# Column sums of w_out: 32 products with ones on TensorE, or 31 additions on VectorE and one product

## The chip, the cores and the metric

One core of a Trainium2 chip. The time is the device time of one execution in microseconds (us). Three runs of the kernel before gave 987.38 us as their median (986.65 to 991.73).

## The reference

Attention over 8 batches of 576 tokens with 8 heads of width 64 gives `x` with 4608 rows of 512. A feed-forward part follows, and the change lies in it:

```python
h = x @ w_in                        # 512 -> 2048
r = np.maximum(h, 0.0)
g = s * (r * r) + b                 # s and b are single numbers
return (g @ w_out).astype(np.float32)   # 2048 -> 512
```

Since `b` is one number, `g @ w_out` is `s * ((r*r) @ w_out)` plus a row of 512 that is the same for every token: `b` times the column sums of `w_out`. The kernel computes this row once, as the tile `bias`.

## The kernel before

`w_in` and `w_out` arrive as 64-bit floats. `split_w(p)` loads the part of them that belongs to f pair `p` (256 of the 2048 hidden columns, `p` = 0 to 7) and turns every number into a high and a low part: `wi[p]` and `wo[p]`. The tile `wo[p]` is 128 partitions by 2 (high, low) by 2 by 512, so it holds four pieces of 128x512. The tokens are tiled in 18 blocks `t` of 256, and each has a high and a low part `xh`, `xl`.

A step `(t, p)` has two halves. `gemm1(t, p)` does 24 products of 256 columns into the PSUM tile `ph` (lines 544 to 546). Then ScalarE does relu, square and a rounded copy `gh` (lines 554 to 556), and VectorE subtracts to get the rest `gl` (line 557). `gemm2(t, p)` does 12 products of 512 columns into two banks `po` (line 582 and 583 use `gh`, line 584 uses `gl`). It comes two steps later in the program, three from `t` = 3 on. In steps 14 to 23 every `ph` lies in bank 4, so the next `gemm1` can begin only when `gl` of the step in front has been read out of `ph`.

The steps run in the order of the list `order`: first `p` = 0 to 6 for `t` = 0 and 1 (steps 0 to 13), then `p` = 0 to 6 for `t` = 2 (steps 14 to 20), then `p` = 7 for the three (steps 21 to 23), then `t` = 3 to 17. The splits of the weights stand at the steps in `CONVERT_AT`, the last one (`p` = 7) at step 11. The attention of later batches is a generator that is advanced by `advance` between the steps. Its head pairs of batches 0 to 2 (`first_unit`) use `sa`, `sl`, `tp`, `tr`, `up` and `ol` products on TensorE, `L382` to `L400` and `L423` on VectorE and `L403` copies on ScalarE; `L271` waits for the load of `tqk`. From batch 3 on `local_unit` loads `lqk` and multiplies on GpSimd (line 455). A scheduler then places all instructions on the engines' queues, and each queue is worked off in that order.

`column_sums` is called ahead of `gemm2(0, 7)`: 32 products of a tile of ones with the pieces of all eight `wo[p]`, added up in bank 5 (`cs`, line 563), so that each of the 128 rows of `cs` holds the column sums. Line 565 multiplies by `b`. The outputs of a block `t` are `s * po + bias` (line 594; line 589 for the last block).

Of the kernel before, what the change touches and what calls it, by code (L numbers as in the profile page):

```python
# [10 lines left out]
F32 = mybir.dt.float32  # L11
F32R = mybir.dt.float32r
# [3 lines left out]
ALU = mybir.AluOpType  # L16
AX = mybir.AxisListType

P = 128
# [18 lines left out]
NFP = DFF // 256  # L38
# [14 lines left out]
HF = 7  # L53
# [8 lines left out]
def attention_ffn_kernel(ctx, tc, qk, vw_in, vr_in, vdm, qkn, vn, w_in, w_out, s_in, b_in, out):  # L62
    nc = tc.nc
    PS = bass.MemoryType.PSUM

    cst = ctx.enter_context(tc.tile_pool(name="cst", bufs=1))
# [4 lines left out]
    def bank(i, shape, name):  # L71
        return ps.tile(shape, F32, tag=f"k{i}", name=name)
# [90 lines left out]
    QV = NQ * 2 * GQ + P  # L163


    ones = cst.tile([P, P], F32R, name="ones")
    nc.gpsimd.memset(ones.bitcast(F32), 1.0)
    bias = cst.tile([P, DM], F32, name="bias")
    eps = cst.tile([P, 1], F32, name="eps")
    nc.gpsimd.memset(eps, 4e-9)  # L170
# [20 lines left out]
    wi, wo, wst = {}, {}, {}  # L191
# [4 lines left out]
    def load_w(p):  # L196

        parts = (("i", src_i[:, :, 512 * p : 512 * p + 512]), ("o", src_o[:, 2 * p : 2 * p + 2]))
        for op, src in parts:
            st = one.tile([P, 1024, 2], I32, tag=f"w{op}{STAGE[p]}", name="wst")  # L200
            nc.sync.dma_start(st.rearrange("p (k f) t -> p k (f t)", k=src.shape[1]), src)
            wst[(p, op)] = st
# [32 lines left out]
    def split_w(p):  # L235
        with tc.high_priority(offset=-BEHIND.get(p, 0)):
            split_parts(p)
# [279 lines left out]
    def split_x(t):  # L517
        tags = ("os", "xl2") if t == 2 else ("xh", "xl")
        pool = one if t == 2 else two
        xh = pool.tile([P, HP, TB], F32R, tag=tags[0], name="xh")  # L520
        xl = pool.tile([P, HP, TB], F32R, tag=tags[1], name="xl")
        t0 = t * TB
        while t0 < (t + 1) * TB:
            b = t0 // S
            while (b, HP - 1) not in complete:
                next(gen)
            n = min((t + 1) * TB, (b + 1) * S) - t0
            src = xt[b][:, :, t0 - b * S : t0 - b * S + n]
            dst = slice(t0 - t * TB, t0 - t * TB + n)
            nc.scalar.copy(xh[:, :, dst], src)  # L530
            nc.vector.tensor_tensor(
                xl[:, :, dst], src, xh[:, :, dst].bitcast(F32), ALU.subtract)
            t0 += n
        xs[t] = (xh, xl)
# [4 lines left out]
    def gemm1(t, p):  # L539
        xh, xl = xs[t]  # L540
        ph = bank(6 if t >= 3 and p % 2 else 7 if t == 1 and p < HF else 4, [P, 2, TB], "ph")
        for j, k in itertools.product(range(2), range(NK)):
            f = slice(P * j, P * j + P)
            nc.tensor.matmul(ph[:, j], wi[p][:, 0, k, f], xh[:, k], start=(k == 0), stop=False)  # L544
            nc.tensor.matmul(ph[:, j], wi[p][:, 0, k, f], xl[:, k], start=False, stop=False)  # L545
            nc.tensor.matmul(ph[:, j], wi[p][:, 1, k, f], xh[:, k], start=False, stop=(k == NK - 1))  # L546
        if t >= 3 and p % 3 == 2:
            both = one.tile([P, 2, 2, TB], F32R, tag="xl2", name="gb")
            gh, gl = both[:, 0], both[:, 1]
        else:  # L550
            gh = two.tile([P, 2, TB], F32R, tag="gh", name="gh")
            gl = two.tile([P, 2, TB], F32R, tag="gl", name="gl")
        with tc.high_priority():
            nc.scalar.activation(ph, ph, AF.Relu)  # L554
            nc.scalar.activation(ph, ph, AF.Square)  # L555
            nc.scalar.copy(gh, ph)  # L556
            nc.vector.tensor_tensor(gl, ph, gh.bitcast(F32), ALU.subtract)  # L557
        gt[(t, p)] = (gh, gl)

    def column_sums():  # L560
        cs = bank(5, [P, DM], "cs")
        for p, i in itertools.product(range(NFP), range(4)):
            nc.tensor.matmul(cs, ones, wo[p][:, i // 2, i % 2],
                             start=(p + i == 0), stop=(p == NFP - 1 and i == 3))
        nc.vector.tensor_scalar(bias, cs, sb_b, None, ALU.mult)

    def gemm2(t, p):
        if (t, p) == (0, NFP - 1):
            column_sums()
        gh, gl = gt.pop((t, p))  # L570
        if p == 0:
            ob = OB.get(t, OB[0])
            oacc[t] = [bank(i, [P, DM], "po") for i in ob]
        po = oacc[t]
        end = t == NB - 1 and p == NFP - 1
        os_ = one.tile([P, 2, DM], F32, tag="os", name="os") if p == NFP - 1 else None
        for m in range(2):
            ms = slice(P * m, P * m + P)
            for j in range(2):
                first = p == 0 and j == 0  # L580
                last = p == NFP - 1 and j == 1
                nc.tensor.matmul(po[m], gh[:, j, ms], wo[p][:, 0, j], start=first, stop=False)  # L582
                nc.tensor.matmul(po[m], gh[:, j, ms], wo[p][:, 1, j], start=False, stop=False)  # L583
                nc.tensor.matmul(po[m], gl[:, j, ms], wo[p][:, 0, j], start=False, stop=last)  # L584
            if end:
                r0 = TB * t + P * m
                for c in (0, DM // 2):
                    cs = slice(c, c + DM // 2)
                    nc.vector.scalar_tensor_tensor(
                        os_[:, m, cs], po[m][:, cs], sb_s, bias[:, cs], ALU.mult, ALU.add)  # L590
                    nc.sync.dma_start(out[r0 : r0 + P, cs], os_[:, m, cs])
        if p == NFP - 1 and not end:
            for m in range(2):
                nc.vector.scalar_tensor_tensor(
                    os_[:, m], po[m], sb_s, bias, ALU.mult, ALU.add)
            nc.sync.dma_start(
                out[TB * t : TB * t + TB, :].rearrange("(m p) c -> p m c", p=P), os_)
# [63 lines left out]
    def advance(st):  # L661
        nonlocal done
        while done < target(st):
            with tc.high_priority(offset=300 if done < NY[1] else 60 if done < NY[1] + NY[2] else 0):
                if next(gen, "end") == "end":
                    break
            done += 1
# [3 lines left out]
    at_step = {st: p + 1 for p, st in enumerate(CONVERT_AT)}  # L671
    for st, (t, p) in enumerate(order):
        gemm1(t, p)
        if st in at_step:
            split_w(at_step[st])
            if at_step[st] + 2 < len(STAGE):
                load_w(at_step[st] + 2)
        advance(st + 0.5)
        pend.append((t, p))
        if len(pend) > (2 if t < 3 else 3):  # L680
            gemm2(*pend.pop(0))
        advance(st + 1)
        if (t, p) in splits:
            split_x(splits[t, p])
# [64 lines left out]
```

## Time and profile before

| what | value |
|---|---|
| median of three runs | 987.38 us |
| profiled execution, its own time | 985.35 us |
| its span (first to last instruction) | 983.5 us |
| TensorE busy | 950.9 us (97%) |
| VectorE busy | 621.6 us (63%) |
| ScalarE busy | 478.0 us (49%) |
| GpSimd busy | 419.0 us (43%) |
| mean granted TensorE clock | 0.989 |

Times inside the execution are counted from the start of the span. PE is TensorE, DVE is VectorE, ACT is ScalarE, POOL is GpSimd and SP issues loads and stores. Matmuls overlap: the record of one is longer than the distance to the next one's start, so the cost of a row of products is read from the distance of the starts. A number in square brackets at the end of a row of the timeline is the idle time of the engine ahead of that row, with what ended it.

### The profile page before, as it was taken

The numbers are of one execution on the slowest core, as the hardware profiler recorded it, in microseconds if no ns is written. First come the engines' busy times: TensorE is split into PE (matmuls) and PEld (weight loads), VectorE is DVE, ScalarE is ACT, GpSimd is POOL, SyncE is SP. The second block draws the span as 40 slices with busy tenths as digits, with TensorE's granted clock in tenths as the row PEclk, the third lists the DMA queues.
The fourth block names the chain that finished last, engine by engine and source line by source line (L and its number), as shares of the span: only waits on it lengthen the run. The fifth ranks groups of instructions, "written<-read, shape, count | busy, mean of one in ns | idle before, by whom it ended". The sixth has DMA issues, their size and how long they took to land.

```text
span 983.5 us, 18562 instructions
## 1 busy us (share of the span) xinstructions
PE 950.9 (97%) x7346; PEld 850.8 (87%) x7346; DVE 621.6 (63%) x1144; ACT 478.0 (49%) x1141; POOL 419.0 (43%) x455
## 2 busy tenths in 40 slices
PE   5769999999999999999999999999999999999998
PEld 4659888788898989898989899999898989898997
DVE  5999985332447697878777976785877771211111
ACT  4878775442555353634455344454445453333231
POOL 9321011000037678676667676575776760000000
PEclk9969999999999999999999999999999999999999
DMA  9746422110323232323232223132323110000000
GB/s 311 259 146 212 138 64 73 48 49 22 122 86 133 67 105 95 126 62 110 72 109 90 90 86 111 34 131 78 113 69 111 54 42 1 22 1 22 1 22 22
DMA packets 32103, 86.27 MB, mean 88 GB/s; under 512 B 3344, under 2 KB 7952, under 8 KB 32016
## 3 DMA queue, kind: packets, MB, share of 16 engines
q1 hardware_dynamic: 32016, 85.08, 26.2%
q8 instruction: 58, 0.95, 0.4%
q14 instruction: 29, 0.24, 0.1%
HBM read 75.63 MB, written 9.44 MB: 86 GB/s over the span
## 4 chain that ended last, share of the span: by engine, by line
PE 80%; DMA 7%; DVE 5%; POOL 3%; ACT 3%; issue 1%; SPq 0%; DVEq 0%; POOLq 0%; ACTq 0%
PE ph L545 12%; PE ph L544 12%; PE ph L546 12%; PE po L582 12%; PE po L583 12%; PE po L584 11%; DMA tqk<-in_qk_dram 4%; PE sa L297 2%; POOL pr L455 2%; PE up L328 1%; PE sl L377 1%; PE ol L420 1%; POOL acc L477 1%; DMA lqk<-in_qkn_dram 1%; PE ot L486 1%
## 5 line engine op out<-in xcount | busy, mean ns | idle before, releaser
L544 PE MATMUL ph<-xh,wi 128*128 128x256 f32 x1152 | 327.7, 285 | 2.2 <-ACT xh L530 2.2
L546 PE MATMUL ph<-xh,wi 128*128 128x256 f32 x1152 | 324.6, 282 | 0.0
L545 PE MATMUL ph<-xl,wi 128*128 128x256 f32 x1152 | 324.4, 282 | 0.0
L455 POOL TENSOR_TENSOR pr<-lqk 128x576 f32<-128x576 f32 x140 | 202.4, 1470 | 87.4 <-DMA lqk<-in_qkn_dram 58.6
L544 PEld LDWEIGHTS ph<-xh,wi 128*128 128x128 f32 x1152 | 217.5, 189 | 8.6 <-ACT xh L530 2.5
L545 PEld LDWEIGHTS ph<-xl,wi 128*128 128x128 f32 x1152 | 217.5, 189 | 5.1 <-issue 0.2
L546 PEld LDWEIGHTS ph<-xh,wi 128*128 128x128 f32 x1152 | 217.8, 189 | 0.6
L554 ACT ACTIVATE ph<-ph 128x512 f32<-128x512 f32 x144 | 83.7, 581 | 255.3 <-PE ph L546 252.1
L582 PE MATMUL po<-wo,gh 128*128 128x512 f32 x456 | 183.3, 402 | 3.4 <-ACT gh L556 3.1
L583 PE MATMUL po<-wo,gh 128*128 128x512 f32 x456 | 182.0, 399 | 0.0
L584 PE MATMUL po<-wo,gl 128*128 128x512 f32 x456 | 178.9, 398 | 0.0
L557 DVE TENSOR_TENSOR gl<-ph,gh 128x512 fp32r<-128x512 f32 x114 | 78.0, 684 | 127.6 <-ACT gh L556 127.5
L477 POOL TENSOR_TENSOR acc<-acc,pv 128x576 f32<-128x576 f32 x80 | 115.5, 1443 | 68.4 <-DVE acc L477 39.2
L457 DVE TENSOR_REDUCE st<-pr 128x9 f32<-128x576 f32 x140 | 105.9, 757 | 43.4 <-POOL pr L455 41.5
L287 POOL TENSOR_TENSOR dq<-vq 64x64 f32<-64x64 f32 x58 | 21.1, 364 | 210.3 <-PE up L326 208.1
L582 PEld LDWEIGHTS po<-wo,gh 128*128 128x128 f32 x456 | 85.9, 188 | 19.4 <-ACT gh L556 4.5
L584 PEld LDWEIGHTS po<-wo,gl 128*128 128x128 f32 x456 | 85.7, 188 | 17.2
L556 ACT CAST gh<-ph 128x512 fp32r<-128x512 f32 x114 | 66.8, 586 | 68.9 <-PE po L583 64.2
L583 PEld LDWEIGHTS po<-wo,gh 128*128 128x128 f32 x456 | 86.0, 188 | 15.6
L476 DVE TENSOR_TENSOR pv<-lv,st 128x576 f32<-128x576 f32 x120 | 87.4, 748 | 18.5 <-POOL acc L477 18.1
L555 ACT ACTIVATE ph<-ph 128x512 f32<-128x512 f32 x144 | 83.7, 582 | 3.3
L583 PE MATMUL po<-wo,gb 128*128 128x512 f32 x120 | 48.0, 400 | 0.0
(143 smaller groups left out, 1252.3 us busy)
## 6 DMA issues: line engine op xcount, KB each, us to landing
tqk<-in_qk_dram SPq DMA_DIRECT2D x30, 584.0 KB, 3.9
lqk<-in_qkn_dram SPq DMA_DIRECT2D x20, 768.0 KB, 4.3
lv<-in_vn_dram SPq DMA_DIRECT2D x20, 480.0 KB, 3.5
out_dram<-os SPq DMA_DIRECT2D x17, 512.0 KB, 3.0
wst<-in_moe_w_in_dram SPq DMA_DIRECT2D x7, 1024.0 KB, 6.5
wst<-in_moe_w_out_dram SPq DMA_DIRECT2D x7, 1024.0 KB, 5.2
tvd<-in_vdm_dram SPq DMA_DIRECT2D x29, 160.0 KB, 2.9
tvr<-in_vr_dram SPq DMA_DIRECT2D x29, 128.0 KB, 2.1
```

The costliest lines, as they stand in the source:

```text
L455: nc.gpsimd.tensor_tensor(pr, lqk[:, 0:CH], lqk[:, CH + o : 2 * CH + o], ALU.mult)
L457: nc.vector.tensor_reduce(ls[:, :, o], pr, AX.X, ALU.add)
L476: nc.vector.tensor_tensor(pv, lv[:, o : o + CH], w, ALU.mult)
L477: (nc.vector if o % 3 == 1 else nc.gpsimd).tensor_tensor(acc[:, :, h], acc[:, :, h], pv, ALU.add)
L544: nc.tensor.matmul(ph[:, j], wi[p][:, 0, k, f], xh[:, k], start=(k == 0), stop=False)
L545: nc.tensor.matmul(ph[:, j], wi[p][:, 0, k, f], xl[:, k], start=False, stop=False)
L546: nc.tensor.matmul(ph[:, j], wi[p][:, 1, k, f], xh[:, k], start=False, stop=(k == NK - 1))
L554: nc.scalar.activation(ph, ph, AF.Relu)
L555: nc.scalar.activation(ph, ph, AF.Square)
L582: nc.tensor.matmul(po[m], gh[:, j, ms], wo[p][:, 0, j], start=first, stop=False)
L583: nc.tensor.matmul(po[m], gh[:, j, ms], wo[p][:, 1, j], start=False, stop=False)
L584: nc.tensor.matmul(po[m], gl[:, j, ms], wo[p][:, 0, j], start=False, stop=last)
```

## The change

`ones` becomes a plain float32 tile. A new function `add_rows(p)` adds the four pieces of `wo[p]` to `bias` on VectorE. The first call is for `p` = 7, where the first instruction adds two pieces to each other, and the next two add the others; the seven calls for `p` = 0 to 6 are four additions each. The calls stand behind `gemm1` of steps 13 to 20. `column_sums` is left with one float32 product of `ones` with `bias`, which adds up the 128 partitions.

```diff
-    ones = cst.tile([P, P], F32R, name="ones")
-    nc.gpsimd.memset(ones.bitcast(F32), 1.0)
+    ones = cst.tile([P, P], F32, name="ones")
+    nc.gpsimd.memset(ones, 1.0)
...
+    def add_rows(p):
+        parts = [wo[p][:, i // 2, i % 2].bitcast(F32) for i in range(4)]
+        if p == NFP - 1:
+            nc.vector.tensor_tensor(bias, parts.pop(), parts.pop(), ALU.add)
+        for part in parts:
+            nc.vector.tensor_tensor(bias, bias, part, ALU.add)
+
     def column_sums():
         cs = bank(5, [P, DM], "cs")
-        for p, i in itertools.product(range(NFP), range(4)):
-            nc.tensor.matmul(cs, ones, wo[p][:, i // 2, i % 2],
-                             start=(p + i == 0), stop=(p == NFP - 1 and i == 3))
+        nc.tensor.matmul(cs, ones, bias, start=True, stop=True)
         nc.vector.tensor_scalar(bias, cs, sb_b, None, ALU.mult)
...
     for st, (t, p) in enumerate(order):
         gemm1(t, p)
+        if 2 * HF - 1 <= st < 2 * HF - 1 + NFP:
+            add_rows((NFP - 1, *range(NFP - 1))[st - 2 * HF + 1])
         if st in at_step:
             split_w(at_step[st])
```

The new lines move the line numbers: behind the change the additions are lines 565 and 567, the single product is line 571, its scaling line 572, the `po` products are lines 589 to 591, and the output line 601.

The scheduler orders all queues anew. Three places matter below. The first is VectorE's queue from the end of the last split on. Before, between one `gl` and the next, it held only work of the attention:

```order
L557 TENSOR_TENSOR gl<-ph,gh 128x512
L382 TENSOR_REDUCE sm<-sl 128x6
L383 TENSOR_TENSOR pl<-sl,sm 128x192
L387 TENSOR_REDUCE sm<-pl 128x12
L388 TENSOR_SCALAR sm<-sm 128x12
L389 RECIPROCAL sm<-sm 128x12
L390 TENSOR_TENSOR pl<-pl,sm 128x384
L271 TENSOR_REDUCE qd<-tqk 128x144
L400 STREAM_TRANSPOSE pt<-pl 128x384
L557 TENSOR_TENSOR gl<-ph,gh 128x512
```

Now an addition stands behind nearly every one of these; this is the end of the same stretch, and the row behind it:

```order
L271 TENSOR_REDUCE qd<-tqk 128x144
L567 TENSOR_TENSOR bias<-bias,wo 128x512
L389 RECIPROCAL sm<-sm 128x12
L567 TENSOR_TENSOR bias<-bias,wo 128x512
L390 TENSOR_TENSOR pl<-pl,sm 128x384
L567 TENSOR_TENSOR bias<-bias,wo 128x512
L400 STREAM_TRANSPOSE pt<-pl 128x384
L557 TENSOR_TENSOR gl<-ph,gh 128x512
L567 TENSOR_TENSOR bias<-bias,wo 128x512 x7
```

From `gl` to `gl`, with the first addition (line 565) just ahead of the first `gl`, the six stretches that follow hold 7, 7, 8, 7, 1 and 0 additions; with line 565 that makes 31. The second holds `L423` besides, the third `L423`, `L298` and `L273`, the fourth `L306`, `L382` and `L383`.

The second place is ScalarE's queue in the same stretch. Before, the copies of the attention into `db` stood ahead of the rounded copy `gh` (line 556):

```order
L554 ACTIVATE ph<-ph 128x512
L403 COPY db<-pt 32x12x32 x2
L555 ACTIVATE ph<-ph 128x512
L403 COPY db<-pt 32x12x32 x2
L322 COPY ptr<-tr 64x144
L556 CAST gh<-ph 128x512
L322 COPY ptr<-tr 64x144
```

Now they stand behind it:

```order
L554 ACTIVATE ph<-ph 128x512
L555 ACTIVATE ph<-ph 128x512
L556 CAST gh<-ph 128x512
L322 COPY ptr<-tr 64x144 x2
L403 COPY db<-pt 32x12x32 x4
L410 COPY ups<-up 128x144
```

The third place is TensorE's queue at the column sums. Before:

```order
L546 MATMUL ph<-xh,wi 128x256
L563 MATMUL cs<-wo,ones 128x512 x32
L584 MATMUL po<-wo,gl 128x512
L544 MATMUL ph<-xh,wi 128x256
L545 MATMUL ph<-xl,wi 128x256
```

Now, one `gemm1` later:

```order
L546 MATMUL ph<-xh,wi 128x256
L571 MATMUL cs<-bias,ones 128x512
L591 MATMUL po<-wo,gl 128x512
L589 MATMUL po<-wo,gh 128x512
L590 MATMUL po<-wo,gh 128x512
```

The attention's pieces stand later among the products, too. Ahead of the last `ol` products of the tenth head pair there were 521 `ph` and 244 `po` products, now 546 and 256. Ahead of the last `up` product of the twelfth head pair, the last one of batch 2, there were 696 and 320, now 697 and 328.

## The prediction

> **What bounds the kernel now.** I read the busy shares of the page first, then stretches of time; the chain of waits comes in under term 4.
>
> ```profile
> PE 950.9 (97%) x7346; PEld 850.8 (87%) x7346; DVE 621.6 (63%) x1144; ACT 478.0 (49%) x1141; POOL 419.0 (43%) x455
> ```
>
> ```profile
> 176.00:232.00 56.00, 52.69 (x531) 44.91 (x525) 17.96 (x38) 23.32 (x54) 4.68 (x12) 0.97 0.15 47
> 365.00:800.00 435.00, 434.75 (x2909) 395.10 (x2907) 336.72 (x595) 206.25 (x507) 299.76 (x277) 1.00 0.28 91
> ```
>
> The reader is to see that TensorE is the bound, and by how much. In the first stretch, where the additions will stand, PE is busy 52.69 of 56 us, DVE 17.96 and POOL 4.68: 38.0 us of DVE are free. From 365 to 800 PE is busy 434.75 of 435 us. So a product that is taken from PE's queue ahead of that stretch shortens the kernel, unless something else then becomes late.
>
> The rows of PE at the column sums show what there is to take.
>
> ```profile
> 232.25 7.64 PE L563 MATMUL cs<-wo,ones 128*128 128x512 f32 x32
> 239.73 0.40 PE L584 MATMUL po<-wo,gl 128*128 128x512 f32 x1
> ```
>
> The record of the 32 products says 7.64 us, but ends overlap. From their first start to the next product's start are 239.73 - 232.25 = 7.48 us, 0.234 us each. PE has no idle time on either side, so all of it is on the path.
>
> **Term 1: the products.** One float32 product takes the place of 32. No float32 product of 128x512 is in the trace. The nearest one is `sa`:
>
> ```profile
> 200.06 0.90 PE L297 MATMUL sa<-kd,dq 128*96 128x144 f32 x6
> 200.70 0.38 PE L544 MATMUL ph<-xh,wi 128*128 128x256 f32 x1
> ```
>
> Three float32 products of 144 columns give six records, so each runs as two passes. From 200.06 to 200.70 they take 0.64 us, 0.107 us for a pass of 144 columns. Scaled to 512 columns, two passes are 2 x 0.107 x 512/144 = 0.76 us, and I take 0.8. Bounds: two passes at the price of the removed products are 0.47 us; two at the whole record, 0.90/6 x 512/144 each, are 1.07 us. Term 1 is 0.8 - 7.48 = **-6.7 us** (-7.0 to -6.4). The product waits for the last addition, but by the working below that is done at about 211 us, over 20 us ahead. `ones` is set by the same memset as before: 0.
>
> **Term 2: do the 31 additions fit between the `gl`?** Prices first.
>
> ```profile
> L477 DVE TENSOR_TENSOR acc<-acc,pv 128x576 f32<-128x576 f32 x40 | 35.3, 882 | 6.2 <-POOL acc L477 6.1
> ...
> L531 DVE TENSOR_TENSOR xl<-x,xh 128x1024 fp32r<-128x1024 f32 x12 | 21.6, 1801 | 9.4 <-ACT xh L530 9.4
> ...
> L233 DVE TENSOR_TENSOR wo<-es,wo 128x512 fp32r<-128x512 f32 x14 | 9.5, 690 | 0.1
> ```
>
> Line 233 is the nearest: two float32 operands in SBUF, 512 columns, 690 ns. The additions depend on each other, and a dependent pair starts about 0.03 us behind the end (178.82 + 0.36, then 179.21 in the rows below). With a little overlap elsewhere I take 0.71 us each, 31 x 0.71 = 22.0 us in all, against 38.0 us free. The dearer rows above lie where POOL works, too: line 477 does 576 columns in 882 ns, and line 531 does 1024 in 1801 ns, but in 1.23 us at 227.12 below. That ratio, 1.46, gives the upper bound, 1.01 us.
>
> DVE takes its queue in order, so the total isn't the question. The question is whether each `gl` (line 557) comes in time, since PE can't start the next `ph` before it.
>
> ```profile
> 178.07 0.69 DVE L557 TENSOR_TENSOR gl<-ph,gh 128x512 fp32r<-128x512 f32 x1 [0.64 <-ACT gh L556]
> 178.82 0.36 DVE L382 TENSOR_REDUCE sm<-sl 128x6 f32<-128x192 f32 x1
> 179.21 0.36 DVE L383 TENSOR_TENSOR pl<-sl,sm 128x192 f32<-128x192 f32 x1
> 180.16 0.55 DVE L387 TENSOR_REDUCE sm<-pl 128x12 f32<-128x384 f32 x1 [0.59 <-ACT pl L386]
> 180.75 0.17 DVE L388 TENSOR_SCALAR sm<-sm 128x12 f32<-128x12 f32 x1
> 180.96 0.23 DVE L389 RECIPROCAL sm<-sm 128x12 f32<-128x12 f32 x1
> 181.22 0.56 DVE L390 TENSOR_TENSOR pl<-pl,sm 128x384 f32<-128x384 f32 x1
> 182.55 0.75 DVE L271 TENSOR_REDUCE qd<-tqk 128x144 f32<-128x576 f32 x1 [0.77 <-DMA tqk<-in_qk_dram]
> 183.22 0.57 DVE L400 STREAM_TRANSPOSE pt<-pl 128x384 f32<-128x384 f32 x1
> 187.20 0.69 DVE L557 TENSOR_TENSOR gl<-ph,gh 128x512 fp32r<-128x512 f32 x1 [3.41 <-ACT gh L556]
> 194.25 0.46 DVE L423 TENSOR_TENSOR x<-ol,ups 128x288 f32<-128x288 f32 x1 [6.37 <-PE ol L420]
> 196.34 0.69 DVE L557 TENSOR_TENSOR gl<-ph,gh 128x512 fp32r<-128x512 f32 x1 [1.62 <-ACT gh L556]
> ...
> 201.00 0.60 DVE L298 TENSOR_REDUCE dmx<-sa 96x3 f32<-96x432 f32 x1 [3.56 <-PE sa L297]
> 201.52 0.74 DVE L273 TENSOR_REDUCE kd<-tqk 128x144 f32<-128x576 f32 x1
> 204.62 0.69 DVE L557 TENSOR_TENSOR gl<-ph,gh 128x512 fp32r<-128x512 f32 x1 [2.35 <-ACT gh L556]
> 205.22 0.16 DVE L306 RECIPROCAL dsm<-dsm 96x3 f32<-96x3 f32 x1
> ...
> 212.65 0.69 DVE L557 TENSOR_TENSOR gl<-ph,gh 128x512 fp32r<-128x512 f32 x1
> ...
> 220.52 0.69 DVE L557 TENSOR_TENSOR gl<-ph,gh 128x512 fp32r<-128x512 f32 x1 [4.03 <-ACT gh L556]
> ...
> 227.12 1.23 DVE L531 TENSOR_TENSOR xl<-x,xh 128x1024 fp32r<-128x1024 f32 x1 [2.21 <-ACT xh L530]
> ```
>
> From one `gl` to the next DVE now has 9.13, 9.14, 8.28, 8.03 and 7.87 us. What stands in each after the change, `gl` itself (0.69) included:
> - First: seven additions 4.97, the eight attention rows 3.55 (0.36, 0.36, 0.55, 0.17, 0.23, 0.56, 0.75, 0.57): 9.2 us. It fits with nothing to spare.
> - Second: seven additions and line 423: 6.1 us.
> - Third: eight additions 5.68, and 0.46 + 0.60 + 0.74: 8.2 us.
> - Fourth: seven additions, and 0.16 + 0.36 + 0.36: 6.5 us.
> - Fifth: one addition, 0.7 us more than now.
>
> So at the old pace every stretch holds what is put into it, and cost of the additions on PE's path is **0**, hidden under PE's own products. If that cover were gone, each 0.1 us of an addition's price would delay `gl` by 0.7 to 0.8 us in each of the four full stretches.
>
> **Term 3: the waits on PE that the new order takes away.** The old pace is slower than PE's own work. A piece of the chain of waits is one product at its pace:
>
> ```profile
> 278.54 0.23 PE po L582
> ...
> 279.73 0.12 PE ph L544
> ```
>
> So the 24 `ph` and 12 `po` products of a step need 24 x 0.12 + 12 x 0.23 = 5.6 us, where `gl` comes every 8 to 9 us. What held PE up is in these rows.
>
> ```profile
> 187.22 0.62 PE L582 MATMUL po<-wo,gh 128*128 128x512 f32 x1 [2.07 <-ACT gh L556]
> ...
> 190.19 0.59 PE L544 MATMUL ph<-xh,wi 128*128 128x256 f32 x1
> ```
>
> ```profile
> 183.82 1.04 ACT L403 COPY db<-pt 32x384 f32<-32x384 f32 x2 [0.16 <-DVE pt L400]
> ...
> 186.59 0.58 ACT L556 CAST gh<-ph 128x512 fp32r<-128x512 f32 x1
> ```
>
> ```profile
> 188.00:190.00 2.00, 2.00 (x8) 1.74 (x7) 0.00 (x0) 0.00 (x0) 0.25 (x1) 0.50 0.00 0
> ```
>
> PE stood 2.07 us for `gh`, whose cast sat at 186.59 behind the copies into `db` that had waited for DVE's row at 183.22. Then the granted clock was 0.50 from 188 to 190. That alone loses half of 2 us, and with the edges on both sides I put the loss at 1.6 us. In the new queue the cast stands ahead of these copies. I followed the new queues with the durations above, each instruction behind its queue and its input. The cast ends at about 184.2, so the four `gh` products and `up` run from 184.3 to 186.0. Then `ph` waits for the second `gl`, which DVE, full with additions, starts at 187.3 and ends at 188.0. That wait is 2.0 us and I let it bring the low clock again; but the next `ph` starts at 188.0 and not at 190.19. By the same working the next four `gl` start at 194.7 (196.34 before), 203.1 (204.62), 209.6 (212.65) and 215.5 (220.52): the second stretch is set by PE, the third and fourth by DVE, the fifth by PE again. Of the last 5.0 us some 1.4 are work put off, an `up` and an `ol` that come a step later; so 3.6 are left, and I round term 3 to **-4 us** for the shorter waits of 0.2 to 0.4 us that the old queue still had behind 220. Bounds: 0, if each stretch keeps its old length, and -6, if the new wait at 186 brings no low clock.
>
> [...]
>
> **Term 4: the attention that follows.** PE reaches 365 us with one last wait, and the chain of waits says what stands behind it.
>
> ```profile
> 280.68 0.67 PE ol L420 x12
> ...
> 282.32 5.22 DMA lqk<-in_qkn_dram
> ```
>
> ```profile
> by line: POOL pr L455 21.0%; POOL acc L477 12.2%; DMA lqk<-in_qkn_dram 11.4%; issue 8.7%; DMA tqk<-in_qk_dram 8.0%; DVE st L457 5.3%; DVE pv L476 4.1%; DVE acc L477 3.4%; ACT pd L301 2.9%; POOL dq L286 2.1%; DVE acc L473 1.8%; DVE x L490 1.
> ```
>
> ```profile
> 365.53 0.47 PE L582 MATMUL po<-wo,gh 128*128 128x512 f32 x1 [0.25 <-ACT dsm L305]
> ```
>
> The second fence is the sum by line of the chain between 282.4 and 365. From 282.32 (load of `lqk`, behind the last `ol` of batch 2) to 365 it runs through POOL, loads, DVE and ACT, without PE, and PE waits 0.25 us at its end. So there is no slack: this chain moves by as much as its start does. In the new order one `ph` and eight `po` more stand ahead of the `up` that releases it, 0.12 + 8 x 0.23 = 2.0 us. PE arrives early by terms 1 and 3 and gets 2.0 us of it back as a wait: **+2 us**. Bounds: 0, if DVE's new order shortens the chain as much, and +3.5, if the wait brings the half clock again for some 3 us (1.5 us).
>
> **Sum.** -6.7 + 0 - 4 + 2 = -8.7 us on the profiled execution's 985.35 us (span 983.5, and 1.85 around it): 976.65. That execution is 2.03 us under the median of the runs, 987.38, so I forecast **978.7 us** as the median. The bounds add to -13.0 (974.4) and -2.9 (984.5).
>
> **Rivals.**
> - DVE keeps the old pace. The first stretch has no spare time, and if the others hold theirs too, term 3 is 0: -6.7 + 2 is -4.7, or -6.7 if the wait at 365 shrinks. I put it at 981.7. For it: two full stretches need 9.2 and 8.2 us of 9.13 and 8.28. Against it: the second and fourth do not.
> - The attention stays behind. The tenth pair's `ol` stands 25 `ph` and 12 `po` later, 25 x 0.12 + 12 x 0.23 = 5.8 us. If the twelfth were as late in time, the chain from 282 would start as late as before, and PE would wait out its lead at 365: -6.7 + 5.8 is -0.9, 986.5. Against it: the count for the twelfth shows 2.0.
> - Slower: the additions cost 1.01 us each, 0.30 more. The first stretch then needs 11.3 us of 9.13, the third 10.6 of 8.28, the fourth 8.6 of 8.03: PE idles 5.1 us more at these three `gl`, and the clock falls each time as at 187, for 1.6 us. That is 5.1 + 4.8 - 6.7 + 2 = +5.2 us, 992.6. It decides from about 0.85 us an addition on: then two stretches overrun by 2.2 us together, and with the clock 5.4 us are lost of the 4.7 that terms 1 and 4 leave. For it: rows at that price are in the trace. Against it: POOL works 4.68 us in that stretch. [...]
>
> That the change wouldn't do what it says I leave out: the queues show one product and 31 additions.
>
> **How the numbers follow.** Chances: the forecast (976 to 981) 0.52, DVE at the old pace 0.22, attention behind 0.15, additions dear 0.11. The range takes in the bounds of the sum and the second rival: 974.0 to 986.6. A measurement of this kernel can tell about 0.5%, 4.9 us, from no change. Faster by more than that are the forecast, most of the first rival (0.16) and a little of the second: 0.70. Within it lie the rest: 0.20. Slower: 0.10.
>
> **What would show it.** The product at `cs` should start under 1.1 us ahead of the next one. The additions should read 0.68 to 0.72 us. The second `gl` should start near 187.3, the next `ph` near 188, and the later `gl` 1.5 to 5 us earlier than now. The wait at 365 should grow to about 2 us. I am wrong if waits for line 557 appear on PE at several steps, or if additions read over 0.85 us.

## The result, and the profile after

Four runs of the changed kernel gave 974.84 us as their median (973.93 to 976.3), beside 987.21 us for the kernel before on the same chip (986.65 to 991.73). The ratio is 0.9877, with a 95% interval of 0.9854 to 0.9901: the change made the kernel 1.0 to 1.5% faster. The forecast was 978.7 us. The profiled execution took 974.94 us (span 973.1), 10.4 us less than that of before, at a mean granted clock of 0.982.

The first line is the page's busy times of the changed kernel. The second fence has the two stretches that the prediction began with.

```profile
PE 937.4 (96%) x7316; PEld 840.0 (86%) x7316; DVE 646.8 (66%) x1175; ACT 478.8 (49%) x1141; POOL 425.0 (44%) x455
```

```profile
176.00:232.00 56.00, 55.11 (x559) 47.61 (x560) 39.02 (x71) 25.80 (x58) 7.67 (x12) 1.00 0.15 47
...
365.00:800.00 435.00, 432.62 (x2880) 391.97 (x2879) 338.94 (x589) 204.86 (x508) 294.00 (x268) 1.00 0.27 87
```

PE has 30 instructions less (one product makes two records) and is busy for 13.5 us less. In the first stretch DVE's busy time rose from 17.96 to 39.02 us, and yet PE stands there for 0.9 us instead of 3.3. In the long stretch PE now stands 2.38 us, where it stood 0.25.

Next, PE's timeline at the column sums of the changed kernel:

```profile
230.62 1.02 PE L571 MATMUL cs<-bias,ones 128*128 128x512 f32 x2
231.08 0.80 PE L591 MATMUL po<-wo,gl 128*128 128x512 f32 x1
231.72 0.40 PE L589 MATMUL po<-wo,gh 128*128 128x512 f32 x1
```

The single product has two records. From its start to the second `po` are 1.10 us, of which the first `po` takes 0.23: the product costs 0.87 us in place of 7.48.

DVE's timeline shows the additions (lines 565 and 567) among the attention rows, and seven steps of `gl`:

```profile
176.84 0.68 DVE L557 TENSOR_TENSOR gl<-ph,gh 128x512 fp32r<-128x512 f32 x1
177.44 0.68 DVE L567 TENSOR_TENSOR bias<-bias,wo 128x512 f32<-128x512 f32 x1
178.04 0.35 DVE L382 TENSOR_REDUCE sm<-sl 128x6 f32<-128x192 f32 x1
178.31 0.68 DVE L567 TENSOR_TENSOR bias<-bias,wo 128x512 f32<-128x512 f32 x1
...
184.05 0.57 DVE L400 STREAM_TRANSPOSE pt<-pl 128x384 f32<-128x384 f32 x1
184.55 0.65 DVE L557 TENSOR_TENSOR gl<-ph,gh 128x512 fp32r<-128x512 f32 x1
185.12 5.88 DVE L567 TENSOR_TENSOR bias<-bias,wo 128x512 f32<-128x512 f32 x7
...
191.29 0.68 DVE L557 TENSOR_TENSOR gl<-ph,gh 128x512 fp32r<-128x512 f32 x1
...
193.59 3.58 DVE L567 TENSOR_TENSOR bias<-bias,wo 128x512 f32<-128x512 f32 x5
...
199.19 0.68 DVE L557 TENSOR_TENSOR gl<-ph,gh 128x512 fp32r<-128x512 f32 x1
...
205.47 0.69 DVE L557 TENSOR_TENSOR gl<-ph,gh 128x512 fp32r<-128x512 f32 x1 [0.18 <-ACT gh L556]
...
212.14 0.69 DVE L557 TENSOR_TENSOR gl<-ph,gh 128x512 fp32r<-128x512 f32 x1 [0.28 <-ACT gh L556]
...
219.29 0.68 DVE L557 TENSOR_TENSOR gl<-ph,gh 128x512 fp32r<-128x512 f32 x1
```

The second `gl` starts 7.71 us behind the first, where it was 9.13 before and 9.2 was forecast. An addition that has an instruction of the attention behind it makes room for it after 0.60 us (177.44 to 178.04). In the run of five an addition takes (3.58 - 0.68) / 4 = 0.73 us, in the run of seven (5.88 - 0.68) / 6 = 0.87 us. From the first to the seventh `gl` are 42.45 us, where it was 50.46 (178.07 to 228.53).

ScalarE's timeline in the first of these steps has the cast `gh` ahead of the copies into `db`:

```profile
182.88 0.59 ACT L556 CAST gh<-ph 128x512 fp32r<-128x512 f32 x1
183.61 0.56 ACT L322 COPY ptr<-tr 64x144 f32<-64x144 f32 x2
184.66 2.08 ACT L403 COPY db<-pt 32x384 f32<-32x384 f32 x4 [0.49 <-DVE pt L400]
```

And PE, at the place where it had stood 2.07 us and then ran at half clock:

```profile
184.82 0.66 PE L328 MATMUL up<-ptm,dq 80*128 80x144 f32 x4
185.25 0.39 PE L544 MATMUL ph<-xh,wi 128*128 128x256 f32 x1
```

```profile
186.00:188.00 2.00, 2.00 (x19) 2.00 (x19) 1.93 (x3) 1.00 (x3) 1.87 (x4) 1.00 0.04 8
188.00:190.00 2.00, 2.00 (x21) 1.51 (x19) 1.93 (x3) 1.51 (x3) 1.74 (x2) 1.00 0.18 55
```

There is no wait at all, and the granted clock is 1.00. The last columns of busy time say that POOL worked 1.87 and 1.74 of the 2 us: this is where the seven additions in a row cost 0.87 us each on average. Four of them kept the usual 0.67 to 0.70 us; the fourth to sixth took 0.975, 0.836 and 1.107 us.

The next two views are the chain of waits behind batch 2, and PE's waits from 240 us on (total, times, longest):

```profile
268.50 0.67 PE ol L420 x12
...
270.39 4.54 DMA lqk<-in_qkn_dram
```

```profile
PE ph L544 <- DVE gl L557: 2.4, 2, 1.2
PE ph L544 <- DVE gb L557: 0.4, 1, 0.4
```

The load of `lqk` starts at 270.39 instead of 282.32. PE's waits behind it are 0.39 us at 358.71, 1.24 at 497.94 and 1.11 at 539.65: 2.7 us in place of 0.25.

To tell the removed work from the shorter waits, I compare two points of PE's queue behind equal numbers of products. The first is a block of `sa` behind 149 `ph` and 52 `po`, the second one behind 816 `ph` and 372 `po`. The kernel before has them in these rows, and the changed kernel in those of the second fence:

```profile
104.58 0.90 PE L297 MATMUL sa<-kd,dq 128*96 128x144 f32 x6
...
308.99 0.90 PE L297 MATMUL sa<-kd,dq 128*96 128x144 f32 x6
```

```profile
104.08 0.90 PE L297 MATMUL sa<-kd,dq 128*96 128x144 f32 x6
...
295.33 0.90 PE L297 MATMUL sa<-kd,dq 128*96 128x144 f32 x6
```

Between the points the change gains (308.99 - 104.58) - (295.33 - 104.08) = 13.2 us. Of these 6.6 are the products (7.48 - 0.87), so 6.6 are something else. PE's idle time between the points fell by 1.7 us only, from 3.80 (204.41 less 200.61 busy) to 2.13 (191.25 less 189.12). By my estimate the low clock of before cost at most another 1.7: it was 0.86, 0.50 and 0.78 in the three windows of 2 us from 186 to 192, a loss of 2 us x (0.14 + 0.50 + 0.22).

The other 3 us or so lie in a place of PE's queue that neither the three places of the section on the change nor the prediction include: the `sl` products of the attention. The first fence is before, the second one after the change:

```profile
172.21 0.24 PE L377 MATMUL sl<-tqk 64*32 64x32 f32 x2
172.38 0.38 PE L546 MATMUL ph<-xh,wi 128*128 128x256 f32 x1
172.69 0.25 PE L377 MATMUL sl<-tqk 64*32 64x32 f32 x2
```

```profile
172.52 0.59 PE L377 MATMUL sl<-tqk 64*32 64x32 f32 x44
...
176.38 0.26 PE L372 MATMUL sl<-maskb,idb 128*128 128x192 bf16 x1 [1.23 <-DVE pl L383]
```

Before, two `sl` and one `ph` take turns until 175.63, at 0.49 us a turn. Now 44 `sl` run in a row. The whole place, 49 `sl` with 8 `ph` among them, took 4.47 us before (171.53 to 176.00); with 4 `ph` among them it takes 1.95 us now (171.09 to 173.04). Four `ph` are 0.5 us, so 2.0 us are saved. A second such place, from 208.44 on, took 2.15 us with three `ph`, and takes 0.74 now: another 1.0 us. The new wait of 1.23 us at 176.38 is part of the idle time above.

From the second point to the end of the span the lead falls from 13.7 to 10.4 us: 3.3 us are given back.

### The profile page after: what moved, and what is told of

Same layout as the page of the kernel before. It is cut to its first block, busy times and chain, and to the rows that moved or that the text cites. A ratio compares the mean times of both kernels' runs of the same rounds, so it can differ in the third digit from the quotient of the medians.

```text
span 973.1 us, 18535 instructions
## 1 busy us (share of the span) xinstructions
PE 937.4 (96%) x7316; PEld 840.0 (86%) x7316; DVE 646.8 (66%) x1175; ACT 478.8 (49%) x1141; POOL 425.0 (44%) x455
## 4 chain that ended last, share of the span: by engine, by line
PE 76%; DVE 7%; POOL 6%; DMA 6%; issue 3%; ACT 2%; DVEq 0%; SPq 0%; POOLq 0%; ACTq 0%
PE ph L544 12%; PE ph L545 12%; PE ph L546 12%; PE po L589 11%; PE po L590 11%; PE po L591 11%; DMA tqk<-in_qk_dram 3%; POOL pr L455 2%; PE sa L297 2%; DMA lqk<-in_qkn_dram 1%; POOL acc L477 1%; DMA wst<-in_moe_w_out_dram 1%; PE up L328 1%; PE ol L420 1%; PE ot L486 1%
## 5 line engine op out<-in xcount | busy, mean ns | idle before, releaser
L544 PEld LDWEIGHTS ph<-xh,wi 128*128 128x128 f32 x1152 | 217.1, 188 | 12.8 <-DVE gl L557 3.4
L287 POOL TENSOR_TENSOR dq<-vq 64x64 f32<-64x64 f32 x58 | 25.6, 441 | 192.4 <-PE up L326 190.2
```

## The experiments

The theory was that of the prediction: the products give their 6.6 us, and VectorE's additions give the rest as a side effect. They push the transposition `pt` back in VectorE's queue, the scheduler then puts ScalarE's cast ahead of the copies that wait for `pt`, and PE no longer stands for the cast. The rivals were that the second half comes from the removed products, too, or from the additions' place and engine as such, and that the attention behind sets what is kept.

All times in the table are medians in us, with the kernel before on the same chip, and the ratio with its 95% interval. "Stretch" is the time from the first to the seventh `gl` in the profile, as above; "late" is what PE waited from 240 to 800 us for other engines, by the view of waits.

| run | time | before | ratio | stretch | late |
|---|---|---|---|---|---|
| the change | 974.84 | 987.21 | 0.9877 (0.9854 to 0.9901) | 42.45 | 2.7 |
| c5_change_again | 974.70 | 987.37 | 0.986 (0.9821 to 0.9898) | 42.54 | 1.2 |
| e1_one_product_no_adds | 981.07 | 985.64 | 0.9945 (0.9924 to 0.9966) | 50.62 | 1.5 |
| e2_adds_beside_32_products | 980.13 | 985.64 | 0.994 (0.9915 to 0.9964) | 42.42 | 1.8 |
| e3_adds_on_gpsimd | 980.78 | 985.64 | 0.9943 (0.9925 to 0.9962) | 50.37 | 1.8 |
| e4_adds_twice | 981.15 | 985.64 | 0.9951 (0.9928 to 0.9975) | 46.20 | 4.2 |
| e6_copies_on_gpsimd_alone | 985.46 | 987.37 | 0.9983 (0.9963 to 1.0003) | 42.20 | 3.9 |
| e8_first_pair_first | 983.87 | 987.37 | 0.9963 (0.9944 to 0.9982) | 47.91 | 0.2 |
| e9_change_copies_on_gpsimd | 981.70 | 987.37 | 0.9941 (0.9917 to 0.9966) | 42.19 | 8.6 |
| g1_one_pair_copies_alone | 983.21 | 985.85 | 0.997 (0.9951 to 0.9989) | 42.32 | 3.3 |
| g3_change_second_pair_copies | 972.67 | 985.85 | 0.9862 (0.9845 to 0.988) | 43.32 | 0.3 |
| g4_change_first_pair_copies | 976.65 | 985.85 | 0.9908 (0.9882 to 0.9934) | 43.43 | 1.9 |
| f1_batch2_urgency_300 | 974.92 | 985.85 | 0.9885 (0.987 to 0.990) | 45.55 | 0.8 |

### The single product without the additions

```diff
+    nc.gpsimd.memset(bias, 0.0)
...
-        for p, i in itertools.product(range(NFP), range(4)):
-            nc.tensor.matmul(cs, ones, wo[p][:, i // 2, i % 2],
-                             start=(p + i == 0), stop=(p == NFP - 1 and i == 3))
+        nc.tensor.matmul(cs, ones, bias, start=True, stop=True)
```

> The bias tile is set to zero and no w_out tile is added up; the single float32 product stays, so the column sums are left out of the output. ScalarE's queue keeps the old order (the copies into db ahead of the cast gh). Theory (products and queue order are two separate gains): only term 1 is left, about 6.7 us, so 979.5 to 981.5 against 987.2, and the wait of about 2 us for gh near 187 with the half clock behind it is still there. Rival (the lead of the earlier steps came from taking the products away, or the additions cost PE time): as fast as the changed kernel or faster, 973 to 976.

Measured: 0.9945, which is 5.4 us of 987. Its timeline of PE has the old wait again, and the window behind it the low clock:

```profile
188.44 0.51 PE L581 MATMUL po<-wo,gh 128*128 128x512 f32 x1 [2.09 <-ACT gh L557]
```

```profile
190.00:192.00 2.00, 2.00 (x11) 2.00 (x10) 0.00 (x0) 0.28 (x1) 1.13 (x4) 0.50 0.00 0
```

Its two `sa` points lie at 105.88 and 303.79, so between them it gains 204.41 - 197.91 = 6.5 us. That is the products' 6.6 and nothing else; the stretch of the seven `gl` is as long as before (50.62). So the removal of the products doesn't bring the shorter waits.

### The additions without the removal

```diff
     for st, (t, p) in enumerate(order):
         gemm1(t, p)
+        if 2 * HF - 1 <= st < 2 * HF - 1 + NFP:
+            add_rows((NFP - 1, *range(NFP - 1))[st - 2 * HF + 1])
```

The 32 products stay, and overwrite the sum of the additions.

> The 32 products stay and give the result; the 31 additions are made as well and their sum is overwritten. ScalarE's queue has the new order (cast ahead of the copies). Theory: the additions cost nothing on PE's path and bring the new order, so the kernel is faster than before although it only does more work: 4 to 5 us, 982 to 983.5. The wait for gh near 187 is gone. Rival (additions cost time that the saved products paid for): 988 to 992; rival (additions neutral): 987.

Measured: 0.994, or 5.9 us faster than before, with 31 instructions more and none less. ScalarE's timeline has the new order:

```profile
183.47 0.59 ACT L556 CAST gh<-ph 128x512 fp32r<-128x512 f32 x1
...
185.25 2.08 ACT L403 COPY db<-pt 32x384 f32<-32x384 f32 x4 [0.48 <-DVE pt L400]
```

PE has no wait at that place, and the stretch is 42.42 us. The `sl` products stand together here as in the change (44 in a row at 173.32). The two halves add: 5.4 + 5.9 = 11.3 us, beside the change's 12.1 (1.23% of 987). So the second half of the gain comes from the presence of the additions on VectorE and the order of the queues that goes with it, not from what they spare.

### The additions on GpSimd

```diff
-            nc.vector.tensor_tensor(bias, bias, part, ALU.add)
+            nc.gpsimd.tensor_tensor(bias, bias, part, ALU.add)
```

The addition of two pieces moves in the same way.

> The same 31 additions on GpSimd in place of VectorE, one product. GpSimd does 576 columns in 1.43 us, so about 1.3 us each, 40 us in all between 176 and 270, where it is nearly idle. ScalarE's queue has the copies into db ahead of the cast again. Theory (the new queue order makes the second gain): it loses most of that gain, 978 to 981. Rival (VectorE's load of additions holds PE back): without that load it is faster than the change, 972 to 974.

Measured: 0.9943, as without additions. ScalarE's timeline has the copies ahead of the cast again, PE waits for it, and the windows show POOL at the additions:

```profile
183.91 2.07 ACT L403 COPY db<-pt 32x384 f32<-32x384 f32 x4 [0.72 <-DVE pt L400]
186.01 0.58 ACT L556 CAST gh<-ph 128x512 fp32r<-128x512 f32 x1
```

```profile
186.65 0.50 PE L589 MATMUL po<-wo,gh 128*128 128x512 f32 x1 [2.26 <-ACT gh L556]
```

```profile
186.00:188.00 2.00, 1.35 (x7) 1.18 (x8) 0.69 (x1) 1.03 (x3) 1.85 (x2) 1.00 0.00 0
188.00:190.00 2.00, 2.00 (x19) 2.00 (x18) 0.00 (x0) 0.28 (x1) 1.67 (x4) 1.00 0.00 0
```

The stretch is 50.37 us though the clock stayed at 1.00. So the low clock alone doesn't make the old pace. The first `sl` products stand together here, too (44 in a row at 173.51), and between the `sa` points, at 105.59 and 302.01, the gain is 8.0 us: 1.4 more than the products. The kernels with a stretch over 47 us (before, e1, e3 and e8) all have the copies ahead of the cast.

### Every addition twice

```diff
-        for part in parts:
+        for part in parts + parts:
```

> Every addition behind the first one of p = 7 and the pieces of each pair is made twice (61 additions, so the sums come out too large by about a factor of 2). That is about 20 us more on VectorE between 176 and 240. Theory (the additions are hidden as long as each stretch between two gl holds them): the cover ends here, waits of PE for gl appear at several steps, 3 to 8 us slower than the change, 978 to 983. Rival (there is cover for twice as many): within 1 us of the change, 974 to 976.

Measured: 981.15 us, 6 to 7 us above the change (0.9951 against 0.9877). The window of its first stretch:

```profile
176.00:232.00 56.00, 53.16 (x477) 45.34 (x477) 50.26 (x89) 26.11 (x59) 6.81 (x12) 0.97 0.12 40
```

DVE is now busy 50.26 of 56 us, and the stretch is 46.20 us. The time lies in the expected range, but not by the expected waits for `gl` at several steps: from 176 to 240 PE waited only 0.2 us for a `gl`. It waited 1.3 us for `pl`, as in the change, and 1.3 us for the cast, 1.1 of them at 225.07, where two copies stand ahead of the cast again. The last `up` of batch 2 also came 3.8 us of products later in PE's queue than in the change (163.1 us of `ph` and `po` products ahead of it against 159.3, counted at an estimated 0.1195 and 0.2317 us each, where the starts of neighbours in PE's rows lie 0.12 and 0.23 us apart), the load of `lqk` started at 286.5 instead of 270.4, and PE waited 4.2 us behind. So thirty more additions cost some 0.2 us each, all their effects on the other queues included; thirty-one cost nothing that can be seen.

### The change once more

> The changed kernel once more, as the reference for the other three runs on this chip. If the first comparison holds, 0.9877 of the kernel before; if part of it was the spread of the kernel before, whose runs lie between 984.6 and 991.7, nearer to 0.989 to 0.990.

Measured: 0.986, and a second profile of the same kernel. Its `sa` points lie at 105.75 and 297.39, a gain of 12.8 us between them (13.2 above). With the same 6.6 for the products, the rest is worth 6.2 us here. Its end is 10.3 us ahead of before's, so from a lead of 11.6 it gave back 1.3.

### The copies on GpSimd, for one pair and for all of batch 2

Without any addition, only the cast is set free: the copies of line 403 leave ScalarE.

```diff
-            nc.scalar.copy(bd[ws, :, ws], pt[ws])
+            if b == 2:
+                nc.gpsimd.tensor_copy(bd[ws, :, ws], pt[ws])
+            else:
+                nc.scalar.copy(bd[ws, :, ws], pt[ws])
```

> The kernel before with its 32 products and no additions; only the copies into db of batch 2's head pairs go from ScalarE to GpSimd, so the cast gh is never queued behind them. Theory (the second gain is the cast that no longer waits behind the copies): the wait of 2 us near 187 and what follows it go, the rows of gl near 196 to 228 come 3 to 8 us earlier, and the kernel is 3 to 6 us faster than before, about 981. Rival (the gain is made by the other moves of the queues, such as sl products that no longer alternate with ph): under 1.5 us faster, 984 to 986.

For g1 the condition is `(b, hp) == (2, 0)`, the pair whose copies stood ahead of the cast.

> The kernel before, 32 products and no additions; only the copies into db of the first head pair of batch 2, those that held the cast near 187, are on GpSimd. The last up product of batch 2 stands 5.6 us of products later than before (it was 11.1 us when all four pairs' copies moved). Theory (the freed cast makes the lead, and a late end of batch 2 gives it back through the load of lqk): the rows of gl lead by 7 to 9 us near 228, less is given back than with all pairs moved, and the kernel is 3 to 5 us faster than before. Rival (the lead is lost whatever the place of the last up): 1 to 2 us faster, as with all pairs.

Measured: the stretch shrank to 42.20 and 42.32 us, just as in the change, with no addition in the kernel. That the order of cast and copies makes the stretch short is shown by this: in both kernels the first `sl` products take turns with `ph` as before. Between the `sa` points (104.96 and 302.75) g1 gains 6.6 us, 0.7 of them because an `up` comes later. But the time fell only by 0.17% (interval from 0.37% faster to 0.03% slower) and 0.3%. The three longest waits of PE in e6 from 240 us on say where part of it went:

```profile
PE ph L548 <- DVE xl L534: 1.5, 1, 1.5
PE ph L547 <- ACT xh L533: 1.2, 1, 1.2
PE ot L489 <- POOL acc L480: 0.8, 1, 0.8
```

In e6 the scheduler put the last `up` of batch 2 behind 168.4 us of products (157.3 before, 159.3 in the change), so the load of `lqk` started at 289.5, later than before's 282.3 in spite of the lead. In g1 it stood behind 162.9 us, and the load started at 282.4; PE then waited 3.3 us for three `gl`. e6 misses what the theory expected, and g1 reaches its lower edge at best. Both gave most of their lead back behind 240 us, as in the prediction's term 4. But the place of the last `up` doesn't settle how much: in e2 it stands behind the same 162.9 us of products as in g1, the load of `lqk` starts at 282.4 in both, the second `sa` point lies at 302.77 beside 302.75, and yet PE waited 1.8 us behind it in e2 and 3.3 in g1. The intervals of the two ratios overlap (up to 0.9964 in e2, from 0.9951 in g1).

### The first pair first

The additions begin with `p` = 0, and the addition of two pieces stands there.

```diff
-        if p == NFP - 1:
+        if p == 0:
...
-            add_rows((NFP - 1, *range(NFP - 1))[st - 2 * HF + 1])
+            add_rows(st - 2 * HF + 1)
```

> The change with the additions in the order p = 0 to 7. Since they all go through one tile, p = 7 first holds all of them back until the last split is done; with p = 0 first the scheduler puts additions early, into the stretch from 25 to 125 us where VectorE is busy 95%. Theory (free VectorE time is what hides them, and the place decides): slower than the change by 4 to 10 us, 979 to 985. Rival (the place doesn't matter, PE hides them anywhere): within 1 us of the change.

Measured: 0.9963, some 9 us slower than the change. With the order of the change, all additions hang on the first, and that one needs the last split, so they can't start ahead of 176 us. Beginning with `p` = 0 they are free early, and the scheduler puts them from 47.8 us on, beside the splits. There VectorE has no room in any of the kernels (behind the length of the window stand PE, PEld and DVE; this is the kernel before):

```profile
25.00:125.00 100.00, 86.25 (x991) 75.15 (x990) 98.14 (x198) 80.79 (x188) 20.93 (x29) 0.91 0.55 184
```

```profile
25.00:125.00 100.00, 82.42 (x974) 71.87 (x975) 98.81 (x195) 73.31 (x174) 19.30 (x24) 0.86 0.55 184
```

The second window is e8's: DVE can hardly be busier, and PE is busy for 3.8 us less than before; in the change it was 84.38 us, so 2.0 us less than there. At the second `sa` point, 305.89, e8 is 10.6 us behind the change. (The `sa` row at 111.22 has 155 `ph` and 72 `po` ahead of it, so it is not the first point.) And the old wait for the cast was back, 1.84 us at 193.06. So beginning with the last f pair carries most of the gain: it holds the additions back until VectorE has time.

### The change with the copies on GpSimd

The edit of e6 on top of the change, then that for the first pair alone (`(2, 0)`, g4) and for the second pair alone (`(2, 1)`, g3).

> The change with the copies into db of batch 2 on GpSimd, too. Theory (cast and copies are already apart in the changed kernel): nothing left to gain, within 1.5 us of the change, 973.5 to 976.5. Rival (ScalarE still holds PE up): 2 us or more faster.

> The change with the copies of the first head pair of batch 2 on GpSimd; the last up product stands where it does in the change. Theory: within 1.5 us of the change. Rival: 981 to 983.

> The change with the copies into db of the second head pair of batch 2 on GpSimd; the last up product stands where it does in the change. Theory (no copy holds a cast in the changed kernel, and where the last up stands decides what is kept): within 1.5 us of the change. Rival (any copy on GpSimd costs the 7 us that moving all of them did): 981 to 983.

Measured: with all copies moved 981.70 us, some 7 us worse than the change, though the stretch is 42.19. Neither the theory nor the rival had that. PE's waits from 240 us on, the three longest:

```profile
PE ph L547 <- DVE gl L560: 5.1, 4, 1.6
PE ph L548 <- DVE xl L534: 1.4, 1, 1.4
PE ph L547 <- ACT xh L533: 1.2, 1, 1.2
```

The last `up` stood behind 163.0 us of products instead of 159.3, and the lead was paid back in these waits. With the first pair's copies alone the time was 976.65, with a wait of 1.4 us at an `up` and 1.9 us behind 240; its `sa` point of 104.58 came at 106.88, so it was behind ahead of the edit, and the cost of moving the pair isn't settled by it.

With the second pair's copies alone it was **972.67 us** (971.67 to 973.73), the best of all, 2.2 us under f1, whose runs on the same chip lie from 974.61 to 975.16. (The change itself did not run on that chip.) This is outside the 1.5 us of the theory, to the fast side, and g4 is just outside it to the slow side. POOL does these copies here:

```profile
211.83 2.18 POOL L404 COPY db<-pt 32x384 f32<-32x384 f32 x4 [22.87 <-DVE pt L400]
```

```profile
PE ph L547 <- DVE gb L560: 0.3, 1, 0.3
```

The second fence is PE's one wait from 240 us on: of the change's late waits only this is left. Why these copies on GpSimd take the others away wasn't followed up.

### Batch 2 more urgent

```diff
-            with tc.high_priority(offset=300 if done < NY[1] else 60 if done < NY[1] + NY[2] else 0):
+            with tc.high_priority(offset=300 if done < NY[1] else 300 if done < NY[1] + NY[2] else 0):
```

> The change with the scheduler's urgency for batch 2's attention raised from 60 to 300; the last up of batch 2 keeps its place, that of the second pair comes 4.8 us of products earlier. Theory (only the end of batch 2 counts): within 1.5 us of the change, 973 to 976.5. Rival (an earlier second pair shortens the stretch): 2 us or more faster.

Measured: 974.92 us, the change's own time. The late waits fell to 0.8 us, but PE now stood 1.1 us at an `ol`, 0.8 at a `ph` and 0.6 at two `po` between 176 and 240, and the stretch is 45.55 us. What the urgency spares behind 240 it costs ahead of it.

## Why the prediction was right, and where it was off

- **What bounds.** Right: PE is the bound, and what is taken ahead of 365 us reaches the end but for the give-back.
- **Term 1, the products, -6.7.** Right: 0.87 us for the new product, -6.6, and 6.5 between the `sa` points of e1. The scaled rows of `sa` had given 0.8.
- **Term 2, the additions, 0 on PE's path.** Right in its result, wrong in its pitch. I took 0.71 us each. They started 0.60 us apart from an independent instruction behind them, and 0.73 or 0.87 us from one another. The first stretch so needed 7.7 us, not 9.2, and had spare time.
- **Term 3, the waits, -4.** The mechanism is there, but it is only half of what was measured, and this is the term that was mis-sized. Two profiles give -6.6 and -6.2, just past the bound of -6. In the first of them some 3.3 us are shorter waits and the low clock, and some 3 us are the `sl` products that no longer take turns with `ph`, which the prediction put at nothing because it did not look at that place of PE's queue. The step of the working that failed was that of the new queues, which put the second `gl` 9.2 us behind the first (at 187.3) with a 2.0 us wait of PE at 186 and the half clock behind it. It came at 184.55, so the next `ph` started at 185.25, and neither the wait nor the low clock appeared. The next ones came at 191.29 (194.7 forecast), 199.19 (203.1), 205.47 (209.6) and 212.14 (215.5).
- **Term 4, the attention behind, +2.** The size was about right (1.3 and 3.3 us in the two profiles, both inside the bounds), the place was not. I expected one wait at 365; there were 0.4 us at 358.71, and the rest at 497.94 and 539.65, at `gl` steps that nothing in the trace of before had marked. In e6, e9 and g1 batch 2 ends later in PE's queue and the lead goes; but e2 has the same late end as g1 and keeps its lead, so the price by products ahead of the last `up` isn't shown.
- **The sum.** -6.6 - 6.4 + 2.3 = -10.7, beside -10.4 and -10.3 in the two profiles; I had -8.7. That is 1.7 us of the 3.9 by which the median missed. The other 2 us are the step from the profile to the median: I added the 2.03 us by which before's profiled execution lay under its runs, and the changed kernel's profiled execution (974.94) lay at its median. The runs of before scatter from 983.35 to 991.76 over one set of 21, so this step was no better than that.
- **The rivals.** DVE at the old pace: refuted, 42.45 us from the first `gl` to the seventh. The attention behind: there, at the forecast's size and not at the rival's, since the last `up` moved by 2.0 us of products only. Dear additions: one took 1.107 us, and seven in a row 0.87 us each beside POOL, over the 0.85 that I had named as the sign of being wrong; but that stretch held only 6.1 us of work by my count, so no `gl` of these stretches was late. (The overruns at 0.85 us add to 2.1 us by my own rows, not 2.2.) The doubled additions lose the second half of the gain, but not by the rival's late `gl`. I had also written that waits for line 557 at several steps would mean that I am wrong. There were four, 0.2 us at 234.62 and the three behind 240, 2.9 us in all; none lies in a stretch that holds additions (the last one started at 206.08), so that sign was drawn too wide.

What stays open: why e2 ends 5.9 us ahead of before where g1, with the same stretch and the same end of batch 2, ends 3 us ahead; and what takes the late waits away in g3. How the scheduler comes to put the cast ahead of the copies was not followed either; the runs only show that it does so with the additions on VectorE and not with the same additions on GpSimd.

## What to carry to other kernels

Work that moves from the bound to an engine with idle time has two effects, what it takes off the bound and where the scheduler puts everything else; build each half alone before you believe a sum, since here adding work by itself was worth as much as taking it away. An in-order queue is read for what stands ahead of the instruction that the bound waits for: four copies ahead of one cast cost more than thirty-one additions (a stretch of 50.46 us with the copies ahead, 42.42 with the additions and the cast ahead). Read every queue that was reordered, TensorE's own too: about half of what the new order gave here lay there, outside the three places that the prediction went by. And look at what holds a chain of accumulations back: the same sum, begun with the first piece instead of the last, ran where its engine was full (98.81 of 100 us) and lost most of the gain.

## What the runs showed of the hardware

- **VectorE overlapped independent neighbours.** An addition of 688 ns (the median of 30) let an independent instruction start after 0.60 us (177.44 to 178.04), a dependent addition after 0.73 us (the five in a row at 193.59).
- **Beside a busy GpSimd some additions were dearer.** Seven in a row took 0.87 us each on average where POOL was busy 1.87 and 1.74 of 2 us, the longest 1.107 us; five in a row took 0.73 us at 193.59, where POOL was idle. The three dear additions end at 188.27, 189.14 and 190.28, each 0.54 or 0.55 us behind the end of a row of GpSimd (187.72, 188.59, 189.74). On GpSimd line 283 took 0.91 us there and 0.47 at 219.79, line 282 1.18 and 0.74. What couples the two engines was not shown.
- **Behind a wait of about 2 us the granted clock fell at one time and not at another.** Behind 2.07 us (before) and 2.09 us (e1) it was 0.50 in the window from 188 to 190 and from 190 to 192, behind 2.26 us (e3) it stayed at 1.00. What decides it was not shown.
- **Where `sl` and `ph` products took turns, PE lost time.** Before, a `ph` between two pairs of `sl` took 0.31 us (172.38 to 172.69) instead of 0.12, and a pair of `sl` 0.17; in the change 44 `sl` in a row took 0.52 us (172.52 to 173.04).
- **The float32 product of 128x512 cost 0.87 us**, 3.7 times the 0.234 us of the products that it replaced.
